# Attention mixing in four array quarters and two PSUM banks, with new order tables, in a fused recurrence and feed-forward kernel

## Chip, cores and metric

One core of a Trainium2 chip. The metric is the device time of one execution in microseconds, the median of three runs. Beside it there is one profiled execution, from which every row below comes. The engines are TensorE (PE; its weight loads are shown apart, PEld), VectorE (DVE), ScalarE (ACT), GpSimd (POOL) and SyncE (SP), which issues most DMAs.

## What is computed

A linear recurrence for each batch and head, then a feed-forward layer with a squared relu. All inputs are float32.

```python
# r, k, v, w: (B, H, S, D) = (4, 8, 768, 48); u: (8, 48)
for t in range(S):
    cur = einsum('bhd,bhe->bhde', u[None] * k[:, :, t], v[:, :, t])
    y[:, :, t] = einsum('bhd,bhde->bhe', r[:, :, t], state + cur)
    state = w[:, :, t, :, None] * state + einsum('bhd,bhe->bhde', k[:, :, t], v[:, :, t])
x = y.transpose(0, 2, 1, 3).reshape(B * S, H * D)          # (3072, 384)
h = maximum(x @ w_in, 0.0)                                 # w_in: (384, 2048)
out = h * h @ w_out                                        # w_out: (2048, 384)
```

## The kernel before

The time axis is cut into six chunks (c) of 128 steps. A chunk of one batch (b) is a unit; there are 24. The eight heads of a unit are four pairs (p): head j=0 of a pair lies in partitions 0 to 47, head j=1 in 64 to 111 (J = 64, HP = 112).

**Attention of a unit** (`attention`). The inputs w, k, r arrive in "st", v in "v". In chunk 0 TensorE transposes them (L466); later VectorE transposes 32x32 blocks and SyncE spreads them by DMA into "pt". VectorE takes the running product of w (L478), ScalarE its inverse (L485, L486), VectorE scales r and k by them. GpSimd and VectorE make beta, the diagonal term from u, and ScalarE writes it as diagonals into two "m" tiles (L515). TensorE makes the scores of each head into the two banks "a" (`scores`, L526), and VectorE copies them under a causal mask into the "m" tiles (L530). Then comes the mix: `inter` multiplies r by the state S (L552, from chunk 1 on) and `part` the masked scores by v (L560), both added up in one "a" bank. ScalarE and VectorE take the result out of the bank, negated and split into a rounded high part and a low rest (L591, L592), into x, the input of the feed-forward products. The 96 rows of pair 1 (`SPLIT`) don't fit beside the other three pairs in 128 partitions: they go to "x3", and six DMAs for each two units (`send`, L599) put them into the 16-row gaps of x. The transposed k (L538) times v gives the state's update (`outer`, L611, "dS"), added by VectorE and scaled by GpSimd (L617 to L620).

An L552 product has 48 rows of contraction and 48 or 64 output columns, so it uses a quarter of the 128x128 array: rows by the side of its head, columns by where its output lies. Before, head j=0 has the first row half and the first column half, j=1 the second of both: two of four quarters. L560 has all 128 rows and one column half. L526 has one row half and all columns.

**Feed-forward** (`ffn`). For each chunk and each of 16 slices (f) of 128 hidden values: nine products L640 (three blocks of 128 inputs, three pairings of high and low parts) into an "hp" bank, over 512 columns or, in chunk 0 and part of chunk 1, twice 256; relu on ScalarE, square on VectorE, high part on ScalarE, rest on VectorE (L645 to L649) into one of three "g" buffers; three products L655 for each batch, added up over all f in one of four "ob" banks. After the last f, ScalarE copies each "ob" to one of two "q" buffers (L660), and a DMA stores it (L662). The eight PSUM banks are thus four "ob", two "hp", two "a".

**Weights.** For each of eight groups, five DMAs bring the rows of w_in in the order that x needs (`load_w`), one brings w_out, and ScalarE, VectorE and GpSimd split them into high and low parts (`split_w`), through the same "q" buffers.

**Order.** Each piece is added to a `Plan` with an engine, a cost, a rank, and what it reads and writes. `Plan.order` is a list scheduler: of the steps that can start first, it takes the one of lowest rank, gives it buffers from named pools, and changes of the array's division cost `SWITCH`. The ranks come from the number tables in `Ranks`. In the first 110 us of the plan it fills TensorE's planned idle time with transposes of an identity (L681). The instructions are then emitted in that order, engine by engine.

**Flag.** Values of w far below the usual would make the fast path inexact; ScalarE adds up such cases in "far" (L518). After the plan, VectorE reduces it, a product with a 128x128 matrix of ones spreads it (L694), and every engine loads the result and branches over a slow path (L698) that does not run here.

## Time and profile before

| | |
|---|---|
| median of three runs | 550.34 us (550.27 to 550.54) |
| the profiled execution | 549.26 us, of which the span from first to last instruction is 547.3 |
| granted TensorE clock | 0.996 of full speed, mean over the span |
| DMA | 50.88 MB in 206456 packets, mean 93 GB/s |
| L640 products | 222.7 us busy |
| L655 products | 226.9 us busy |
| L526, L552, L560, L611 products | 28.3, 38.8 (21.5 + 17.3 by shape), 27.2 and 22.9 (12.4 + 10.5) us busy; these overlap each other in part |

A row of the profile's groups has the line, the engine, the operation, what it writes and reads, the shapes, the count, then the busy time in us and the mean of one in ns, then the idle time of the engine just before it and what ended that. In the timeline, a row has the start and the length in us of a run of like instructions, and in brackets the idle time before it. A matmul's end is modelled and lies after the start of the next one, so costs are best read from start to start. Weight loads overlap the products.

### The profile page before, as it was taken

To read this page: it belongs to the slowest core of one execution; us is meant where nothing else is said; L and a number is where in the kernel's file an instruction comes from. 1 tells how busy PE (TensorE), PEld (TensorE's weight loads), DVE (VectorE), ACT (ScalarE), POOL (GpSimd) and SP (SyncE) were. 2 spreads that over 40 slices of the span, in tenths; PEclk is the share of its full clock that TensorE was granted. 3 is DMA by queue.
4 is the path that set the end of the run, shared out by engine and by line. 5 is a ranking of instruction groups with operands and counts; after the bars stand their busy time and mean duration, and the time that the engine had idled before them with its cause. 6 is when DMAs were issued, how large, how long until landed. Compare 5 with 4: busy or idle time off the path is not lost. (4 is left out here: it accounts for less than half of the span.)

```text
span 547.3 us, 10350 instructions
## 1 busy us (share of the span) xinstructions
PE 532.6 (97%) x3930; PEld 474.5 (87%) x3930; DVE 357.1 (65%) x650; ACT 287.3 (52%) x677; POOL 102.3 (19%) x119
## 2 busy tenths in 40 slices
PE   7899999999999999999999999999999999999995
PEld 6778988889998989888888888888888889899994
DVE  5889989999587775958667747656855332333331
ACT  2886885566855845655643654545553332332322
POOL 5335653540212020210302002003000000000000
PEclk9999999999999999999999999999999999999998
DMA  9999699156563825455553723703411000000001
GB/s 164 216 244 272 128 245 206 24 90 136 115 132 64 169 47 105 97 104 99 101 107 62 138 73 60 142 3 73 74 57 30 1 0 16 29 31 1 0 1 62
DMA packets 206456, 50.88 MB, mean 93 GB/s; under 512 B 196161, under 2 KB 201281, under 8 KB 206401
## 3 DMA queue, kind: packets, MB, share of 16 engines
q1 hardware_dynamic: 205680, 49.17, 44.0%
q10 hardware_dynamic: 720, 0.98, 0.6%
q8 instruction: 33, 0.54, 0.4%
q14 instruction: 23, 0.18, 0.1%
HBM read 31.65 MB, written 4.72 MB: 66 GB/s over the span
## 5 line engine op out<-in xcount | busy, mean ns | idle before, releaser
L655 PE MATMUL ob<-wo,g 128*128 128x384 f32 x1152 | 226.9, 341 | 0.5 <-ACT g L648 0.5
L640 PE MATMUL hp<-x,wi 128*128 128x512 f32 (+1 forms) x1062 | 222.7, 355 | 1.4 <-DVE g L649 0.9
L655 PEld LDWEIGHTS ob<-wo,g 128*128 128x128 f32 x1152 | 199.3, 188 | 9.2 <-ACT g L648 0.7
L640 PEld LDWEIGHTS hp<-x,wi 128*128 128x128 f32 x1062 | 174.5, 188 | 27.5 <-DVE g L649 2.3
L645 ACT ACTIVATE t<-hp 128x512 f32<-128x512 f32 (+1 forms) x118 | 61.1, 518 | 154.2 <-PE hp L640 132.5
L646 DVE SCALAR_TENSOR_TENSOR hp<-hp,t 128x512 f32<-128x512 f32 (+1 forms) x118 | 70.3, 596 | 102.0 <-ACT t L645 101.5
L649 DVE TENSOR_TENSOR g<-hp,g 128x512 fp32r<-128x512 f32 (+1 forms) x118 | 68.9, 585 | 38.1 <-ACT g L648 37.3
L648 ACT CAST g<-hp 128x512 fp32r<-128x512 f32 (+1 forms) x118 | 59.5, 505 | 55.7 <-DVE hp L646 55.6
L515 ACT ACTIVATE m<-ident,beta 128x128 f32<-128x128 f32 x192 | 60.4, 395 | 1.2 <-DVE beta L508 1.2
L505 POOL TENSOR_TENSOR st<-st 128x384 f32<-128x384 f32 x24 | 26.6, 1108 | 61.7 <-DVE st L432 54.5
L620 POOL TENSOR_TENSOR S<-S,Ec 112x192 f32<-112x192 f32 x16 | 8.3, 523 | 142.2 <-DVE S L619 142.2
L530 DVE COPY_PREDICATED m<-caus,a 128x512 f32<-128x512 uint8 x48 | 33.3, 730 | 0.7 <-PE a L526 0.6
L478 DVE TENSOR_TENSOR_SCAN pt<-pt,zero 112x128 f32<-112x128 f32 x80 | 30.3, 426 | 3.0 <-DMA v<-in_v_dram 1.3
L526 PEld LDWEIGHTS a<-pt 48*128 48x128 f32 x384 | 23.6, 187 | 7.3 <-issue 5.1
L526 PE MATMUL a<-pt 48*128 48x128 f32 x384 | 28.3, 285 | 1.1 <-DVE pt L498 1.1
L560 PE MATMUL a<-m,v 128*48 128x128 f32 (+1 forms) x384 | 27.2, 279 | 1.0 <-DVE m L530 1.0
L432 DVE STREAM_TRANSPOSE st<-st 128x1152 f32<-128x1152 f32 x20 | 27.2, 1366 | 0.0
L560 PEld LDWEIGHTS a<-m,v 128*48 128x48 f32 (+1 forms) x384 | 20.0, 128 | 6.4 <-issue 4.6
L592 DVE SCALAR_TENSOR_TENSOR x<-a,x 112x128 fp32r<-112x128 f32 (+2 forms) x44 | 17.5, 431 | 12.3 <-ACT x L591 11.7
L507 POOL TENSOR_TENSOR st<-st,un 128x384 f32<-128x384 f32 x24 | 25.1, 1047 | 1.6
L404 POOL TENSOR_TENSOR wi<-q,wi 128x768 fp32r<-128x768 f32 x8 | 17.6, 2204 | 38.0 <-ACT wi L403 31.5
L495 DVE TENSOR_TENSOR pt<-pt,m 112x512 f32<-112x512 f32 x24 | 17.4, 728 | 8.9 <-ACT m L486 8.3
(78 smaller groups left out, 417.1 us busy)
## 6 DMA issues: line engine op xcount, KB each, us to landing
pt<-st SPq DMA_DIRECT2D x80, 96.0 KB, 2.3
ro<-in_moe_w_out_dram SPq DMA_DIRECT2D x8, 768.0 KB, 7.5
v<-in_v_dram SPq DMA_DIRECT2D x24, 192.0 KB, 3.4
st<-in_w_dram SPq DMA_DIRECT2D x11, 384.0 KB, 4.2
st<-in_k_dram SPq DMA_DIRECT2D x11, 384.0 KB, 5.4
st<-in_r_dram SPq DMA_DIRECT2D x11, 384.0 KB, 5.6
pt<-st SPq DMA_DIRECT2D x80, 48.0 KB, 2.5
out_dram<-q SPq DMA_DIRECT2D x20, 192.0 KB, 1.9
```

What stands on the lines that cost most here:

```text
L432: V.transpose(out=zt[:, i].rearrange("a t p q i -> a t (p q) i"), in_=sv[:, :, i].rearrange("s t p q x -> s t (p q) x"))
L478: lambda p=p: V.tensor_tensor_scan(out=pt[:, 0, p], data0=src(0)[:, p], data1=zero.broadcast_to([HP, C]), initial=1.0, op0=ALU.mult, op1=A ...
L515: A.activation(mv(j)[:, p], ident, AF.Copy, scale=beta.tile[:, 2 * p + j:2 * p + j + 1])
L526: T.matmul(mts[j].tile.rearrange("s (p t) -> s p t", p=NP)[:, p], pt[js, 2, p], pt[js, 1, p], start=True, stop=True)
L530: lambda j=j: V.copy_predicated(out=mv(j), mask=caus.unsqueeze(1).broadcast_to([128, NP, C]), data=mts[j].tile.rearrange("s (p t) -> s p t ...
L560: T.matmul(ybv()[to:to + n + D, spot(p)], vt.tile[:, o - n:o + D], mv(j)[:, p], start=(c == 0 and p == SPLIT), stop=True, skip_group_check ...
L640: T.matmul(hp.tile[:, 0:n], wi[f][:, wl, kt], xT[:, kt, xl, xs], start=(m == 0), stop=(m == 3 * KT - 1))
L645: P.add("act", 0.5 if full else 0.28, rank("g"), lambda: A.activation(t(), h(), AF.Relu), r=[hp], w=[(g, 1)])
L646: P.add("dve", 0.61 if full else 0.33, rank("g"), lambda: V.scalar_tensor_tensor(out=h(), in0=h(), scalar=0.0, in1=t(), op0=ALU.max, op1=A ...
L648: P.add("act", 0.53 if full else 0.31, rank("g"), lambda: A.copy(out=hi(), in_=h()), r=[hp], w=[(g, 0)])
L649: P.add("dve", 0.61 if full else 0.33, rank("g"), lambda: V.tensor_tensor(out=lo(), in0=h(), in1=hi().bitcast(F32), op=ALU.subtract), r=[h ...
L655: T.matmul(obs[b][:, 0:DM], g.tile[0][:, gl, o:o + C], wo[f][:, wl], start=(f == 0 and m == 0), stop=(f == NF - 1 and m == 2))
```

## The change

- The mix has two "a" banks (`yb`, `far_yb`) from chunk 1 on. Pairs 3 and 1 (`ACROSS`) put their heads' outputs in the other column half and into the second bank, so the eight L552 products of a unit go through all four quarters in turn. The outputs are taken out by three copies on each of ScalarE and VectorE in place of two and two, and `send` takes its rows from the other sides.
- The rows of w_in follow: the 96-row piece of each group is loaded as two of 48, so six DMAs in place of five, eight more in all. The slow path is adapted in the same way.
- The state update may only come after the mix (`after=[mixed]`).
- The planner lets a step ask ahead for slots that a later step will need (`claim`), and when a pool runs short it keeps the free place for the waiting step of lowest rank that lacks only that pool. The planned cost of the mix is 1.45 in place of 1.94.
- In the last chunk, the four results go to four "m" buffers; ScalarE copies batches 0 and 2, VectorE batch 1, and each half of batch 3; batches 0 and 2 are stored from ScalarE's queue, 1 and 3 from SyncE's.
- The flag is made by planned steps, with a product of one column, in place of steps after the plan.
- All tables in `Ranks` have new numbers.

```diff
-    AT = {'load': -105.75, 'z': 279.5, ...
-    LAG = 2
+    AT = {'load': -139.75, 'z': 137.75, ...
+    LAG = 74.5
...
+    ACROSS = (3, 1)
...
-        pieces = (..., (raw[PC:128 - PC, 2], rows[KT * R:KT * R + R]),
+        pieces = (...,
+                  (raw[PC:J, 2], rows[KT * R + D:KT * R + R]), (raw[J:HP, 2], rows[KT * R:KT * R + D]),
...
-        P.add("pe", 1.0, rank("mt"), scores, r=RK + KK, w=mts, mode=1)
+        P.add("pe", 1.0, rank("mt"), scores, r=RK + KK, w=mts, mode=1, claim=Ms)
...
         yb = Slot("a")
+        far_yb = Slot("a") if c else yb
+        side = lambda p, j: 1 - j if p in ACROSS else j
+        ahead = lambda p, j: PC if p in TILES and side(p, j) == 0 else 0
+        def spot(p):
+            if c == 0:
+                return ybv()[:, TILES.index(p) if p in TILES else KT]
+            return ybv(far_yb)[:, ACROSS.index(p)] if p in ACROSS else ybv()[:, TILES.index(p)]
         def inter():
-            for p in (*TILES, SPLIT):
+            for p in (0, 3, 2, 1):
                 for j in range(2):
-                    js, n = slice(j * J, j * J + D), ahead(p, j)
-                    T.matmul(ybv()[j * J:j * J + n + D, spot(p)], Ss[b][js, PC + p * D - n:PC + p * D + D], pt[js, 1, p],
-                             start=(spot(p) == 0), stop=False, skip_group_check=True)
+                    js, n, to = slice(j * J, j * J + D), ahead(p, j), side(p, j) * J
+                    T.matmul(spot(p)[to:to + n + D], Ss[b][js, PC + p * D - n:PC + p * D + D], pt[js, 1, p],
+                             start=(p in (0, 3)), stop=False, skip_group_check=True)
...
-            P.add("pe", 1.94, rank("mix"), mix, r=[vt, *Ms, ("S", b), *RK], w=[yb], mode=3)
-            outs = [("x", lambda: ybv()[0:HP, 0:KT], ..., xk, 0.4, 0.47),
-                    ("x3", lambda: ybv()[0:HP, KT], ..., (x3, ui), 0.18, 0.21)]
+            mixed = P.add("pe", 1.45, rank("mix"), mix, r=[vt, *Ms, ("S", b), *RK], w=[yb, far_yb], mode=3, claim=[x3])
+            outs = [("x", yb, lambda: ybv()[0:HP, 0:2], ..., xk + (0,), 0.3, 0.34),
+                    ("x", far_yb, lambda: ybv(far_yb)[0:HP, 0], ..., xk + (1,), 0.18, 0.21),
+                    ("x3", far_yb, lambda: ybv(far_yb)[0:HP, 1], ..., (x3, ui), 0.18, 0.21)]
...
-            P.add("pe", 0.5, rank("dS"), outer, r=[vt, Kt], w=[dS], mode=3)
+            P.add("pe", 0.5, rank("dS"), outer, r=[vt, Kt], w=[dS], mode=3, after=[mixed] if c else [])
...
-                os_ = Slot("q")
-                P.add("act", 0.4, rank("os"), ... A.copy(out=os_.tile[:, 0:DM], in_=obs[b][:, 0:DM]), r=[("ob", b)], w=[os_])
-                q_, e = ("actq", nc.scalar) if c == NC - 1 else ("sp", nc.sync)
+                end = c == NC - 1
+                os_ = Slot("m" if end else "q")
+                cut = DM // 2 if end and b == B - 1 else DM
+                if end and b % 2:
+                    P.add("dve", 0.45, rank("os"), ... V.tensor_copy(out=os_.tile[:, 0:cut], in_=obs[b][:, 0:cut]), ...)
+                else:
+                    P.add("act", 0.4, rank("os"), ... A.copy(out=os_.tile[:, 0:DM], in_=obs[b][:, 0:DM]), ...)
+                if cut < DM:
+                    P.add("act", 0.25, rank("os"), ... A.copy(out=os_.tile[:, cut:DM], in_=obs[b][:, cut:DM]), ...)
+                q_, e = ("actq", nc.scalar) if end and not b % 2 else ("sp", nc.sync)
...
+    P.add("dve", 0.2, rank, bad, r=[("far", c, b) for c in range(NC) for b in range(B)], w=["flag"])
+    P.add("pe", 0.2, rank, lambda: T.matmul(fps.tile[0:1, 0:1], flag, one, start=True, stop=True), r=["flag"], w=[fps])
...
-    fps = pas[0][:, 0:1]
-    T.matmul(fps, ones, flag, start=True, stop=True)
```

Three places in the order show what moves. The first is on TensorE, the L552 products of batch 1 in chunk 3 before (a_145 and a_146 are the two "a" banks, pt_127 holds the transposed r, S_130 the state of batch 1; the size is output rows by columns):

```order
L552 MATMUL a_146<-pt_127,S_130 64x128
L552 MATMUL a_146<-pt_127,S_130 48x128
L552 MATMUL a_146<-pt_127,S_130 64x128
L552 MATMUL a_146<-pt_127,S_130 48x128
L552 MATMUL a_146<-pt_127,S_130 64x128
L552 MATMUL a_146<-pt_127,S_130 48x128 x3
```

and the same eight products now, at line 564 of the changed kernel:

```order
L564 MATMUL a_145<-pt_127,S_130 64x128
L564 MATMUL a_145<-pt_127,S_130 48x128
L564 MATMUL a_146<-pt_127,S_130 48x128
L564 MATMUL a_146<-pt_127,S_130 64x128
L564 MATMUL a_145<-pt_127,S_130 64x128
L564 MATMUL a_145<-pt_127,S_130 48x128
L564 MATMUL a_146<-pt_127,S_130 48x128 x2
```

All eight went to one bank; now two go to one and two to the other in turn.

The second place is on TensorE too, behind the mix of the same unit: before, its last four L560 products (m are the masked scores, v_151 its v) and the first of a state update, that of batch 3 of chunk 2, whose v is v_152:

```order
L560 MATMUL a_146<-m_156,v_151 64x128
L560 MATMUL a_146<-m_158,v_151 48x128
L560 MATMUL a_146<-m_156,v_151 48x128
L560 MATMUL a_146<-m_158,v_151 48x128
L611 MATMUL a_145<-v_152,m_154 64x48
L611 MATMUL a_145<-v_152,m_154 48x48
L611 MATMUL a_145<-v_152,m_154 64x48
```

and now, the last of the mix of batch 1 (v_152) and the first of the state update of batch 0 (v_153); L668 is the former L655, L624 the former L611:

```order
L572 MATMUL a_146<-m_156,v_152 48x128
L572 MATMUL a_146<-m_155,v_152 48x128
L668 MATMUL ob_139<-wo_59,g_99 128x384 x3
L668 MATMUL ob_140<-wo_59,g_99 128x384 x3
L668 MATMUL ob_141<-wo_59,g_99 128x384 x3
L624 MATMUL a_145<-v_153,m_159 64x48
L624 MATMUL a_145<-v_153,m_159 48x48
```

A state update stood right behind the mix, in the bank that the mix left free; now nine feed-forward products on the undivided array stand between them. Through the whole order, TensorE goes from the undivided array to a divided form 60 times in place of 51, and between divided forms 25 times in place of 29. The identity transposes that fill idle time are 120 in place of 130, with 103 in place of 99 ahead of the first feed-forward product.

The third place is the end of ScalarE's work, before:

```order
L660 COPY q_147<-ob_139 128x384
L662 DMA out_dram<-q_147 128x384
L660 COPY q_148<-ob_140 128x384
L662 DMA out_dram<-q_148 128x384
L660 COPY q_147<-ob_141 128x384
L662 DMA out_dram<-q_147 128x384
L660 COPY q_148<-ob_142 128x384
L662 DMA out_dram<-q_148 128x384
```

and now (ob_139 to ob_142 are batches 0 to 3):

```order
L678 COPY m_155<-ob_139 128x384
L682 DMA out_dram<-m_155 128x384
L678 COPY m_157<-ob_141 128x384
L682 DMA out_dram<-m_157 128x384
L680 COPY m_156<-ob_142 128x192
```

Batch 1 and one half of batch 3 have gone to VectorE, and their two stores to SyncE's queue, where they are the last of the main program.

102 lines of the change are left out of this document (55 added, 47 removed).

## Prediction

> **What bounds the kernel now.** I read the page's busy times first, then the stretches of the span, then the waits of TensorE. On the page:
>
> ```profile
> span 547.3 us, 10350 instructions
> PE 532.6 (97%) x3930; PEld 474.5 (87%) x3930; DVE 357.1 (65%) x650; ACT 287.3 (52%) x677; POOL 102.3 (19%) x119
> ```
>
> TensorE is busy for 97% of the span, and no other engine for more than 65%. An average can hide stages, so the span is cut at 35, 100 and 541 us (columns: stretch, then busy time and count of TensorE, its weight loads, VectorE, ScalarE, GpSimd, then the granted clock, DMA share and GB/s):
>
> ```profile
> 0.00:35.00 35.00, 29.65 (x272) 24.89 (x272) 26.99 (x61) 21.43 (x54) 17.22 (x33) 1.00 1.05 207
> 35.00:100.00 65.00, 62.86 (x479) 55.94 (x480) 58.76 (x101) 49.10 (x105) 30.14 (x16) 1.00 0.88 199
> 100.00:541.00 441.00, 440.05 (x3182) 393.63 (x3182) 271.35 (x491) 215.79 (x517) 54.91 (x70) 1.00 0.34 68
> 541.00:547.30 6.30, 0.00 (x0) 0.00 (x0) 0.00 (x0) 0.96 (x2) 0.00 (x0) 0.62 0.31 104
> ```
>
> From 100 to 541 us TensorE is idle for 0.95 us in 441, at full clock: there, a microsecond of TensorE removed is a microsecond of span, as long as nothing new starves it. Before 35 us it idles for 5.35 us and also runs transposes that only fill idle time. After 541 us it has nothing left to do. So there are three stages with three limits: start, body, tail.
>
> ```profile
> L681 PE MATMUL a<-ident 128*128 128x128 f32 x97 | 15.0, 303 | 1.6 <-POOL ident masks.py:199 1.6
> L681 PE MATMUL hp<-ident 128*128 128x128 f32 x33 | 4.5, 276 | 0.0
> 12.21 4.31 PE L681 MATMUL a<-ident 128*128 128x128 f32 x38
> ```
>
> The fillers are 97 + 33 = 130; 38 in a row take 4.31 us, 0.113 us each, so 14.7 us of TensorE's "work" is idle time in disguise, all of it before 100 us.
>
> **The products with the state (body).** One unit in the middle of the body, in order of time (start, length, engine, line, operation, count; each float32 product shows as two records):
>
> ```profile
> 281.26 1.08 PE L552 MATMUL a<-pt,S 48*64 48x128 f32 x16
> 282.28 1.09 PE L560 MATMUL a<-m,v 128*64 128x128 f32 x16
> 283.19 0.62 PE L611 MATMUL a<-v,m 128*48 128x48 f32 x16
> 283.74 2.35 PE L655 MATMUL ob<-wo,g 128*128 128x384 f32 x12
> 285.94 2.26 PE L640 MATMUL hp<-x,wi 128*128 128x512 f32 x9
> ```
>
> From start to start, the 16 records of L552 take 1.02 us and those of L560, after which the array keeps its division, 0.91 us: 8 steps of 0.11 us, with two records in each. A record alone, the filler of the same 128 columns, also takes 0.113 us. So two quarters of the array already work side by side, and the other two are empty in L552 (48 rows by at most 64 columns each). How the pairs run:
>
> ```profile
> L552 PE MATMUL a<-pt,S 48*64 48x128 f32 x1 | 0.3, 320 | 0.0
> L552 PE MATMUL a<-pt,S 48*48 48x128 f32 x1 | 0.3, 307 | 0.0
> L611 PE MATMUL a<-v,m 128*64 128x48 f32 x8 | 0.6, 220 | 0.0
> L611 PE MATMUL a<-v,m 128*48 128x48 f32 x8 | 0.5, 208 | 0.0
> L611 PE MATMUL a<-v,m 128*64 128x48 f32 x2 | 0.3, 222 | 0.0
> ```
>
> The first two rows are the stretch 173.70 to 173.80 by shape: two products in different quarters have started there, although the first product's second record stands between them in the program. The next two are 177.68 to 178.30, eight records of each shape; the last is 178.20 to 178.22, where only the 64-column shape still runs. In the program the 48-column product comes last. So each division of the array takes its own products as fast as it can, past records that wait for another division. With four divisions I expect four records in a step: 4 steps in place of 8, 1.02 - 4 x 0.11 = 0.58 us, a gain of 0.44 us. Twenty units (chunks 1 to 5, four batches) have it: **20 x 0.44 = 8.8 us off**. Bounds: nothing if only two records ever run together; 10.2 us if the whole 1.02 us halves.
>
> Here two rules of the Trainium skill speak against the change. "TensorE: Matmul & The Clock Gate", section "The mechanism" under "Part 3: Packing small matmuls", says that matmuls start and end strictly in program order; by that, a third product would queue behind the second record of the first, and the gain would be 0. The trace does not agree: the 48-column shape of L611 was done while the 64-column one still ran. "TensorEngine Tiling (Array Packing)", "Gotcha 1: PSUM Pressure", says that row tiles cannot access one PSUM bank at the same time; by that, the two quarters that still share a bank would take turns, four records would need two steps, and again the gain would be 0. The trace does not agree here either: the two L552 records that started in one tenth of a microsecond are of the two row halves and write one bank.
>
> **More changes of the array's division (body).** The changed order takes the state update (L611) out of the mix's back and puts feed-forward products between them, as the rows on the change show. Counted through the whole order, TensorE leaves the undivided array 60 times in place of 51, and changes between divided forms 25 times in place of 29. The price, from these rows:
>
> ```profile
> 119.16 0.67 PE L611 MATMUL a<-v,m 128*64 128x48 f32 x16
> 119.76 2.36 PE L640 MATMUL hp<-x,wi 128*128 128x512 f32 x9
> 121.95 2.25 PE L655 MATMUL ob<-wo,g 128*128 128x384 f32 x12
> ...
> 441.87 2.26 PE L640 MATMUL hp<-x,wi 128*128 128x512 f32 x9
> 443.97 2.24 PE L655 MATMUL ob<-wo,g 128*128 128x384 f32 x12
> 446.06 2.26 PE L640 MATMUL hp<-x,wi 128*128 128x512 f32 x9
> 448.25 1.08 PE L552 MATMUL a<-pt,S 48*64 48x128 f32 x16
> 449.26 1.09 PE L560 MATMUL a<-m,v 128*64 128x128 f32 x16
> 450.28 2.03 PE L655 MATMUL ob<-wo,g 128*128 128x384 f32 x10
> ```
>
> Nine L640 take 2.10 us (441.87 to 443.97), but 2.19 before a divided group (446.06 to 448.25) and 2.19 after one (119.76 to 121.95): 0.09 each. L560 takes 0.91 before L611 and 1.02 before L655 (449.26 to 450.28): 0.11. L611 alone takes 0.60, not 0.55: 0.05. Together 0.34 per extra excursion, 9 x 0.34 = 3.0, less 4 x 0.09 for the inner changes: **2.6 us on**. If a third of the extra excursions lie in the start, where TensorE idles anyway, it is 1.7; 3.0 is the upper end.
>
> **Both banks for the mix (body).** The mix now needs both "a" banks, and three copies on ScalarE and three on VectorE empty them in place of two and two:
>
> ```profile
> L591 ACT ACTIVATE x<-a 112x384 fp32r<-112x384 f32 x20 | 9.7, 487 | 8.7 <-PE a L560 7.8
> L591 ACT ACTIVATE x<-a 112x128 fp32r<-112x128 f32 x20 | 5.4, 269 | 1.1 <-PE a L560 1.1
> L592 DVE SCALAR_TENSOR_TENSOR x<-a,x 112x384 fp32r<-112x384 f32 x20 | 11.1, 556 | 7.2 <-ACT x L591 6.7
> L592 DVE SCALAR_TENSOR_TENSOR x<-a,x 112x128 fp32r<-112x128 f32 x20 | 5.6, 282 | 3.5 <-ACT x L591 3.5
> ```
>
> Two of three blocks lie between the rows: about 0.38 us on ScalarE and 0.42 on VectorE. The first bank is free about 0.9 us after the mix, the second after about 0.38 + 0.42 + 2 x 0.28 = 1.4, with hand-overs 1.5. The extra 20 x 0.27 on each engine hides in their idle third and more of the body. What is queued on TensorE behind the mix is mostly feed-forward work that needs no such bank: in the changed order 2 to 5 us of it, 1.57 us (nine L655 of 0.174) in three or four units, 0.52 us in the first unit of chunk 1. I take one wait of 0.4 us and crumbs: **0.5 us on**. Ends: 0, and 3 us if every thin cover is missed by half a microsecond.
>
> **The start.** The order holds 120 fillers in place of 130, so the plan sees less idle time, though 103 in place of 99 ahead of the first feed-forward product. Ten fillers are **1.1 us off**. The splitting of one w_in piece adds eight DMA issues on SyncE's queue; the weights they bring are wanted tens of microseconds later, except the first. VectorE (26.99 of 35 us, then 58.76 of 65) is nearly as full as TensorE here, so the real order of waits decides: from 3 us off to 2 us on.
>
> **The tail.** ScalarE alone empties the last results, through two buffers:
>
> ```profile
> 534.12 6.43 PE L655 MATMUL ob<-wo,g 128*128 128x384 f32 x36
> 539.99 0.48 ACT L660 COPY q<-ob 128x384 f32<-128x384 f32 x1 [0.48 <-PE ob L655]
> 541.47 0.48 ACT L660 COPY q<-ob 128x384 f32<-128x384 f32 x1 [1.00 <-DMA out_dram<-q]
> 542.41 0.48 ACT L660 COPY q<-ob 128x384 f32<-128x384 f32 x1 [0.47 <-SPq L698]
> 542.92 1.02 ACTq L662 DMA_DIRECT2D out_dram<-q  x1
> out_dram<-q ACTq DMA_DIRECT2D x4, 192.0 KB, 2.3
> out_dram<-q SPq DMA_DIRECT2D x20, 192.0 KB, 1.9
> ```
>
> The last products end at 540.55. The third copy waits for the first buffer's DMA; the last issue starts at 542.92, lands by the median 2.3 us later (545.2), and 2.1 us of closing follow. With four buffers and two engines nothing waits for a landing: ScalarE copies batch 2 from about 540.05 to 540.53, issues its DMA until 540.9 (0.36 us, as at 539.53), copies its half of batch 3 until about 541.25 (VectorE's half is done before), and SyncE issues at 541.3, to land 1.9 to 2.3 later and end 2.1 after that: 545.3 to 545.7, so **1.7 us off**. If ScalarE's issue takes 1.02 us as the last one did, 1.0; if landing and closing shrink, 2.4. The flag's product and comparisons, planned into the body, leave a stretch in which they delayed nothing that ended last; I count them at nothing, and at 0.2 us on TensorE if uncovered.
>
> **Sum.** The profiled execution took 549.26 us: its span of 547.3 and 2.0 around it. -8.8 + 2.6 + 0.5 - 1.1 - 1.7 = -8.5, so 540.8. The median of the runs is 1.1 above the profiled one (550.34), which gives **541.8 us** in the median. A tie for a measurement of this kernel is what lies within 0.2%, 549.2 to 551.4.
>
> **Rivals.**
> - **Partial overlap.** Four quarters share one stream of instructions, and a step would have to take four weight loads. L611 issued its 16 records in 0.55 us, 0.034 each, which leaves four in 0.14 us, longer than a step of 0.11; against it, its 64-column shape set that pace. Half of the gain lost: 541.8 + 4.4 = 546.2.
> - **No overlap.** Only two records ever run together; the rows of before show no third. Then 541.8 + 8.8 = 550.6, a tie. (The two rules of the Trainium skill named above would give this.)
> - **Slower: the mix starves on its banks.** Scores before it and transposes behind it need the same two banks. If ScalarE's and VectorE's queues hold the six copies behind feed-forward work, TensorE waits at each mix. It is slower than before by 0.2% from (551.4 - 541.8) / 20 = 0.48 us per mix on; at the whole 1.5 us, it is 541.8 + 30 = 571.8. Against it: the body idles 0.95 us in all, ScalarE and VectorE about half and two fifths of it, and most mixes have 2 us of cover.
>
> **How the numbers follow.** Four quarters at once: 0.68, at 541.8; with the ends of the other terms taken together as roots of squares it reaches from 538.5 to 546. Partial: 0.14, at 546.2. None: 0.12, at 550.6. Starving: 0.06, above 551.4 in most of it. The range must hold 8 in 10: all of the first case but its lowest edge, and the partial one with its own spread, so 538 to 548. Faster by over 0.2%: 0.68 + 0.14 + 0.02 (no overlap, but a good start and tail) = 0.84; same 0.10; slower 0.06.
>
> **What would show it.** Right: L552's successor shows 16 records in about 0.58 us from start to start, and some tenth of a microsecond in which four of them start; TensorE idles under 2 us between 100 us and its end; 2.1 us of closing follow a landing about 3 us after the last product. Wrong on the overlap: the 16 records still take 1.0 us. Wrong on the banks: TensorE's waits name the copies of the mix or the masks. Wrong on the start: the first L640 begins more than 2 us away from its time of before, or fillers and idle time before 100 us add up to more than now.

## The result and the profile after

| | before | after |
|---|---|---|
| median of the runs on this chip | 550.44 us (550.27 to 551.28) | 546.89 us (545.78 to 547.37) |
| ratio of the two, 95% interval | | 0.993 [0.9915, 0.9946] |
| the profiled execution | 549.26 us, span 547.3 | 546.83 us, span 545.1 |

Faster by 0.7%: 3.55 us, where 8.5 were forecast. The time lies inside the forecast range, and well short of the forecast. The page after:

```profile
span 545.1 us, 10409 instructions
PE 525.9 (96%) x3920; PEld 462.0 (85%) x3920; DVE 361.2 (66%) x672; ACT 289.9 (53%) x696; POOL 103.0 (19%) x119
```

TensorE's busy time fell by 6.7 us and the span by 2.2: most of what was taken out of the products has come back as idle time. The span cut into start, body and tail as before (stretch, then busy time and count of TensorE, its weight loads, VectorE, ScalarE, GpSimd, then clock, DMA share, GB/s):

```profile
0.00:35.00 35.00, 28.73 (x271) 23.89 (x271) 28.07 (x59) 20.44 (x46) 18.27 (x33) 1.00 1.06 200
35.00:100.00 65.00, 61.29 (x467) 54.59 (x467) 60.41 (x102) 48.22 (x111) 26.45 (x16) 1.00 0.96 203
100.00:538.10 438.10, 435.89 (x3194) 383.48 (x3183) 272.42 (x512) 220.93 (x539) 58.30 (x70) 1.00 0.43 68
538.10:545.10 7.00, 0.01 (x1) 0.00 (x0) 0.36 (x1) 0.32 (x1) 0.00 (x0) 0.68 0.34 114
```

TensorE idles for 6.27 + 3.71 = 9.98 us before 100 us (7.49 before the change), for 2.21 in the body (0.95 before, of which 0.33 lie behind TensorE's last record, so 0.61 up to it) and for 7.0 in the tail (6.75, from the end of the last product at 540.55). The timeline of TensorE after, at the first mix with a state and at one in the middle (start, length, line, operation, count):

```profile
99.60 0.67 PE L564 MATMUL a<-pt,S 48*64 48x128 f32 x16
100.19 0.98 PE L572 MATMUL a<-m,v 128*64 128x128 f32 x14
...
300.80 2.25 PE L653 MATMUL hp<-x,wi 128*128 128x512 f32 x9
302.98 0.67 PE L564 MATMUL a<-pt,S 48*64 48x128 f32 x16
303.58 1.09 PE L572 MATMUL a<-m,v 128*64 128x128 f32 x16
304.60 0.72 PE L653 MATMUL hp<-x,wi 128*128 128x512 f32 x2
```

The 16 records of the products with the state (now L564) take 0.59 and 0.60 us from start to start, where they took 1.02; 0.58 was forecast. All four quarters run: the first four records start between 302.98 and 303.00. L572 takes 1.02 before an undivided product, as it did. TensorE's waits after (what waits, for whom, us in total, times, longest):

```profile
PE ob L472 <- DMA st<-in_w_dram: 2.2, 3, 1.3
PE a L572 <- DVE m L536: 1.9, 2, 1.1
PE hp L653 <- DVE g L662: 1.8, 4, 1.0
PE a L712 <- POOL ident masks.py:199: 1.6, 1, 1.6
PE a L472 <- DVE S L630: 1.3, 1, 1.3
```

All but the third are of the start: input transposes behind DMAs and behind the state in a bank they need, the mix of chunk 0 behind its mask, and the identity, which came as late before. The third is mostly of the body: feed-forward products behind g. Three of the same waits before:

```profile
PE ob L466 <- DMA st<-in_w_dram: 0.3, 1, 0.3
PE a L560 <- DVE m L530: 1.0, 2, 0.6
PE a L466 <- DVE S L617: 0.3, 1, 0.3
```

Where every microsecond of TensorE went, from the records of the two traces (from each product's start to the next one's, idle time taken out):

| TensorE, us | before | after | difference |
|---|---|---|---|
| r times state (L552, L564) | 20.28 | 12.37 | -7.9 |
| masked scores times v (L560, L572) | 23.87 | 25.26 | +1.4 |
| feed-forward products | 415.06 | 416.92 | +1.9 |
| state update and transposed k | 18.13 | 17.84 | -0.3 |
| fillers | 18.89 | 17.33 | -1.6 |
| idle, up to the last product | 6.49 | 10.59 | +4.1 |
| the flag's product | 0.28 | 0.12 | -0.2 |

The rest of TensorE's work differs by under 0.1. The sum is the 2.6 us by which TensorE's last record ends earlier (before, that is the flag's product).

### The profile page after: what moved, and what is told of

Same layout as the page of the kernel before. It is cut to its first block, busy times and chain, and to the rows that moved or that the text cites. A ratio compares the mean times of both kernels' runs of the same rounds, so it can differ in the third digit from the quotient of the medians.

```text
span 545.1 us, 10409 instructions
## 1 busy us (share of the span) xinstructions
PE 525.9 (96%) x3920; PEld 462.0 (85%) x3920; DVE 361.2 (66%) x672; ACT 289.9 (53%) x696; POOL 103.0 (19%) x119
## 4 chain that ended last, share of the span: by engine, by line
PE 75%; DVE 7%; DMA 6%; SPq 5%; ACT 4%; issue 1%; DVEq 0%
PE hp L653 32%; PE ob L668 31%; PE a L572 4%; PE a L532 3%; DMA ri<-in_moe_w_in_dram 2%; SPq L429 2%; SPq L448 2%; PE a L564 2%; DMA st<-in_w_dram 1%; PE a L624 1%; ACT m L521 1%; PE a L544 1%; DVE st L438 1%; DMA v<-in_v_dram 1%; DVE g L662 1%
## 5 line engine op out<-in xcount | busy, mean ns | idle before, releaser
L668 PE MATMUL ob<-wo,g 128*128 128x384 f32 x1152 | 221.4, 339 | 0.0
L668 PEld LDWEIGHTS ob<-wo,g 128*128 128x128 f32 x1152 | 198.5, 188 | 7.1 <-issue 2.0
L662 DVE TENSOR_TENSOR g<-hp,g 128x512 fp32r<-128x512 f32 (+1 forms) x118 | 68.8, 584 | 33.7 <-ACT g L661 31.7
L605 DVE SCALAR_TENSOR_TENSOR x<-a,x 112x128 fp32r<-112x128 f32 (+2 forms) x64 | 20.1, 344 | 31.4 <-ACT x L604 29.4
L511 POOL TENSOR_TENSOR st<-st 128x384 f32<-128x384 f32 x24 | 25.0, 1041 | 63.6 <-DVE st L438 62.5
L536 DVE COPY_PREDICATED m<-caus,a 128x512 f32<-128x512 uint8 x48 | 34.2, 731 | 4.1 <-PE a L532 4.1
L572 PE MATMUL a<-m,v 128*48 128x128 f32 (+1 forms) x384 | 27.5, 278 | 1.9 <-DVE m L536 1.9
L604 ACT ACTIVATE x<-a 112x128 fp32r<-112x128 f32 (+2 forms) x64 | 18.1, 322 | 19.6 <-PE a L572 18.1
L491 ACT ACTIVATE m<-pt 112x512 f32<-112x512 f32 x24 | 15.2, 633 | 24.6 <-DVE pt L484 20.5
L513 POOL TENSOR_TENSOR st<-st,un 128x384 f32<-128x384 f32 x24 | 26.6, 1112 | 1.8
L572 PEld LDWEIGHTS a<-m,v 128*48 128x48 f32 (+1 forms) x384 | 20.2, 128 | 6.9 <-issue 4.4
L410 POOL TENSOR_TENSOR wi<-q,wi 128x768 fp32r<-128x768 f32 x8 | 16.1, 2018 | 43.3 <-ACT wi L409 24.3
```

Of the source, the lines that this page charges most:

```text
L536: lambda j=j: V.copy_predicated(out=mv(j), mask=caus.unsqueeze(1).broadcast_to([128, NP, C]), data=mts[j].tile.rearrange("s (p t) -> s p t ...
L572: T.matmul(spot(p)[to:to + n + D], vt.tile[:, o - n:o + D], mv(j)[:, p], start=(c == 0 and p == SPLIT), stop=True, skip_group_check=True)
L662: P.add("dve", 0.61 if full else 0.33, rank("g"), lambda: V.tensor_tensor(out=lo(), in0=h(), in1=hi().bitcast(F32), op=ALU.subtract), r=[h ...
L668: T.matmul(obs[b][:, 0:DM], g.tile[0][:, gl, o:o + C], wo[f][:, wl], start=(f == 0 and m == 0), stop=(f == NF - 1 and m == 2))
```

## The experiments

Each kernel is the changed one with the edit that its diff shows, unless another is named. Each group of runs was taken on one chip, beside the kernel before; the chip differs between groups.

### First group: the same again, two quarters, the old tail, stores from ScalarE

**The changed kernel again**, without an edit.

> The changed kernel as it is, so that the others of this call have it on the same chip. Every theory: 546.9 within 0.5 us, 3.5 us under the kernel before.

Measured: 550.66 us median (548.8 to 553.82, 12 runs), before 550.57; ratio 0.9991 [0.9973, 1.0009]. Neither number was expected: on this chip the gain is gone, and the runs spread over 5 us. The mean granted clock of these runs goes from 0.982 to 0.992, that of the four first runs from 0.993 to 0.999, that of the kernel before from 0.993 up in nearly all of its runs. The windows of this run's start (the clock is the third number from the end):

```profile
20.00:25.00 5.00, 3.22 (x26) 2.14 (x24) 4.97 (x9) 2.59 (x6) 2.57 (x2) 0.85 1.18 164
25.00:30.00 5.00, 5.00 (x37) 4.28 (x35) 2.08 (x6) 2.89 (x7) 2.18 (x3) 0.50 1.04 248
...
45.00:50.00 5.00, 3.85 (x30) 2.80 (x30) 4.46 (x8) 4.34 (x10) 2.36 (x2) 0.74 1.00 265
50.00:55.00 5.00, 5.00 (x32) 4.56 (x30) 2.09 (x4) 2.38 (x8) 1.26 (x1) 0.58 1.06 257
```

and of the kernel before, whose start kept the full clock:

```profile
20.00:25.00 5.00, 4.28 (x56) 3.30 (x57) 4.62 (x7) 4.89 (x13) 1.55 (x1) 1.00 1.18 166
40.00:45.00 5.00, 4.41 (x59) 3.52 (x58) 4.62 (x9) 4.34 (x13) 2.52 (x1) 1.00 1.08 222
```

TensorE's clock is halved from 23.5 to 33.7 us and from 47.4 to 54.2, each time after idle time (20.5 to 22.0, and some 1.9 us in pieces between 44 and 46.5). A straight line through the 12 runs says 0.48 us more for each 0.001 of mean clock less (correlation -0.95), and 546.6 us at 0.997, beyond the highest clock among them. Lines through the runs of the kernel before in the first three groups say 550.4 to 550.9 there (one run at 0.947 left out). So with the clock held, the change gains about 4 us, and where it falls in most runs, as on this chip, nothing is left.

Why the same idle time halves the clock in one execution and not in another can be read from all 18 traces. Within a trace, all changes of the clock lie a whole number of 3.41 us apart, and this grid begins elsewhere in each execution (its first change is seen at 4.7 to 7.6 us). Cut at the grid, the 17 stretches in which TensorE idled for 1.73 us or more were all followed by half clock; none with up to 1.20 was; of the 25 between, seven were. Here the gap from 20.5 to 22.0 lies in one stretch, and 1.73 of its 3.41 us are idle:

```profile
20.08:23.49 3.41, 1.68 (x13) 0.89 (x11) 3.38 (x7) 2.51 (x6) 1.06 (x1) 1.00 1.07 165
23.49:26.90 3.41, 3.37 (x26) 2.74 (x27) 1.69 (x3) 0.31 (x1) 1.74 (x2) 0.50 1.26 206
```

In the first profile of the changed kernel a gap of nearly the same length (20.71 to 21.99) is cut in two by its grid at 21.84; 1.13 us fall into the first stretch, and the clock holds:

```profile
18.43:21.84 3.41, 2.28 (x21) 2.04 (x19) 3.41 (x6) 3.38 (x10) 0.00 (x0) 1.00 0.95 147
```

**Two quarters again:** the products keep their order and their two banks, the outputs go back to the own column half (all but pair 1 in chunk 0, where no product with the state is).

```diff
-        side = lambda p, j: 1 - j if p in ACROSS else j
+        side = lambda p, j: 1 - j if c == 0 and p == SPLIT else j
```

with the rows of w_in and of `send` to match.

> The changed kernel with its order, both banks and three copies, but with the state products back in two quarters (head j=0 always in the first column half, w_in rows and sends to match). Theory A, the four quarters give all that their rows show (0.43 us in each of 20 units) and the rest was lost elsewhere: 8.6 us above the changed kernel, about 555.5, with 1.0 us for 16 records. Theory B, the gain is given back because TensorE then waits for something else: 4 us or less above, about 551, with less idle time of TensorE than the changed kernel has between 100 us and its end.

Measured: 555.65 us (552.49 to 556.52), ratio to before 1.0075 [1.0049, 1.0101]. Its timeline:

```profile
279.52 1.08 PE L564 MATMUL a<-pt,S 48*64 48x128 f32 x16
280.53 1.09 PE L572 MATMUL a<-m,v 128*64 128x128 f32 x16
```

The 16 records take 1.01 us again, so the four quarters alone do it, not the second bank or the order. All of them take 20.49 us against 12.37. At a clock of 0.997 the lines through the runs give 552.8 against 546.6: of the 8.1 us that the rows show, 6.2 arrive in the time (5.0 by the medians). That lies between the two theories; 555.65 is theory A's figure only because the changed kernel itself took 3.8 us more here than the 546.9 that it starts from. TensorE idles 1.5 us less in the slower kernel (9.09 to 10.59): this fits theory B's reason, that where products get shorter, waits for others grow.

**The old tail:** the last results through two "q" buffers and ScalarE alone, as before.

> The changed kernel with the last results as before: two buffers, all four copies and stores on ScalarE. Theory A, the new tail is worth nothing, since it ends 7.0 us after the last product where the old one took 6.75: within 0.5 us of the changed kernel. Theory B, the forecast's 1.7 us are in it and the loss lies before: 1.7 us above the changed kernel, 548.6.

**Stores from ScalarE:** all four last stores from ScalarE's queue.

```diff
-                q_, e = ("actq", nc.scalar) if end and not b % 2 else ("sp", nc.sync)
+                q_, e = ("actq", nc.scalar) if end else ("sp", nc.sync)
```

> The changed kernel with all four last stores issued from ScalarE's queue, copies and buffers as changed. Theory A, SyncE's late stores hold up its jump over the slow path, which took 4 us on SyncE and VectorE after the last branch: the closing shrinks and the time is 1 to 3 us under the changed kernel. Theory B, the jump is slow for another reason: within 0.5 us of the changed kernel, SyncE again silent for about 4 us after its branch.

Measured: 550.56 us (546.82 to 553.3) and 549.19 (546.18 to 551.35); at 0.997, 546.1 and 546.4. Neither differs from the changed kernel by more than the lines can tell. From the last product's end to the span's end it is 6.7 and 6.3 us, against 6.8 in the changed kernel's profile of this group and 7.0 in its first: undoing the tail change changes nothing, although its last issue comes 3.05 us after the last product and not 0.77. With all stores from ScalarE, SyncE is past its branch at 481.8 us and nothing of it holds SyncE at the end: it goes on 0.02 us after each of the last two stores has landed. But these land 3.66 and 3.69 us after their issue, so the time is theory B's, and not for theory B's reason.

### Second group: the start

**Fillers where TensorE idled:** 37 more identity transposes, 10 and 11 ahead of two input transposes and 16 ahead of one mix of chunk 0.

```diff
+            if s.engine == "pe" and self.filler:
+                for _ in range({7: 10, 20: 11, 25: 16}.get(k, 0)):
+                    self.filler(s.fill[1] if k < 25 else self.spare)
+                k += 1
```

> The changed kernel once more, as the base for the three others of this call on the same chip. Theory A (the spread of its times comes from TensorE's granted clock in the start): times again from about 546 to 554, and the profile's mean clock and its time lie on one line with the earlier ones, 546.6 at 0.997 and 0.5 us more for each 0.001 less. Rival B (the spread is something of the chip, not of the kernel): spread under 1.5 us here, or a time off that line by over 1.5 us.

> The changed kernel with 37 more identity products (0.11 us each, 4.2 us in all) in the waits at 20 to 23 us and 37 to 43 us of the start, where TensorE idled in short pieces before its clock was halved. Theory A (the broken-up idle time lets the clock fall): the clock is 1.00 in every slice of 5 us before 100 us, the times lie within 1.5 us of each other at 546 to 547, about 3.5 us under the kernel before. Rival B (the fall has another cause): spread and median as in the changed kernel without them (550 with 546 to 554), and half clock is seen again. Rival C (the fillers stand in the way): clock held, but up to 4 us more in every run, 549 to 551.

Measured: the changed kernel again 549.2 us (545.9 to 552.06, 12 runs; ratio 0.9953 [0.9933, 0.9972]; 546.9 at 0.997, 0.44 us for each 0.001), with the fillers 548.6 (547.26 to 549.15, 7 runs; 0.9948 [0.9929, 0.9967]). The start of the run with fillers:

```profile
20.00:25.00 5.00, 4.36 (x47) 3.44 (x47) 4.83 (x9) 2.51 (x6) 2.64 (x2) 1.00 1.21 174
...
40.00:45.00 5.00, 4.78 (x52) 3.64 (x50) 5.00 (x9) 4.97 (x14) 1.81 (x1) 1.00 1.10 175
```

Without fillers, theory A: the same spread, and the profile (552.06 at 0.987) within 0.7 us of the line. With them, full clock up to 100 us in this profile, and a spread of 1.9 us in place of 6.2: fillers in the idle pieces hold the clock, though not always (of three profiles with them, one has half clock from 30.8 to 34.2). But the median is about 2 us over theory A's. Part of it are the fillers themselves (547.7 us at 0.997, 0.8 more than without), and half clock shows up in another place, in the body. TensorE and, below it, VectorE of the same run:

```profile
154.49 1.21 PE L673 MATMUL ob<-wo,g 128*128 128x384 f32 x6
157.97 2.29 PE L658 MATMUL hp<-x,wi 128*128 128x256 f32 x9 [2.27 <-DVE g L667]
160.06 1.16 PE L673 MATMUL ob<-wo,g 128*128 128x384 f32 x3
```

```profile
156.86 0.74 DVE L489 TENSOR_TENSOR_SCAN pt<-pt,zero 112x128 f32<-112x128 f32 x2 [2.51 <-DMA pt<-st]
157.52 0.40 DVE L667 TENSOR_TENSOR g<-hp,g 128x256 fp32r<-128x256 f32 x1
```

VectorE's scans of the next unit wait 2.51 us for the DMA of the transposed w; g, ready long before, is queued behind them; TensorE waits 2.27 us for g, and its next nine products take 2.09 us from start to start, at half clock, in place of 1.06.

**Fillers and stores from ScalarE.**

> As the one with 37 more identity products, and all four last stores issued from ScalarE's queue, so that SyncE has nothing to do after the last product. Theory A (the tail's 7 us are closing work that no copy or issue sets): within 0.5 us of the kernel with the same fillers. Rival B: 1 us or more under it, since the last issue follows the last copy on the same engine.

Measured: 548.1 us (545.52 to 549.14, 6 runs), ratio 0.9932 [0.9909, 0.9956]: as with the fillers alone, within what can be told. It is the lowest median of that group; its interval overlaps that of the changed kernel.

**The old start order:** the tables `U0`, `AT0`, `W0`, `WL` of before, all else new.

> The changed kernel with the four order tables that set the start (U0, AT0, W0, WL) as they were before; it holds 181 fillers and 64 excursions to a divided array. Theory A (the new start order costs the held clock and some 1.3 us more): clock 1.00 before 100 us, times within 1.5 us of each other; in the body the gain of the four quarters stays (20 x 0.42 = 8.4 us less on TensorE), and the time lies between 544 and 549, by how much the 61 more fillers (6.9 us at most) stand for idle time that was there before. Rival B (the start order is not what lowers the clock): half clock is seen in it too, and the times spread over 4 us or more.

Measured: 564.58 us, 1.0254 [1.023, 1.0279]: a miss for both theories. TensorE is busy for only 91.15 us of the 100 from 100 to 200 us, and at 100 to 105 us the clock falls to 0.72. The tables only fit together; half of each set is worse than either, and says nothing on the start alone.

### Third group: VectorE's queue, and the price of a division

**g ahead of the scans** at the two places in chunk 2 where TensorE waits for it (155 and 187 us), on VectorE alone but for one cast and one activation on ScalarE that change places. Rows of VectorE's order at the first place, t, hp and g being the feed-forward's, pt and m the next unit's:

```diff
-pt_127<-pt_127,zero 112x128 x2
 g_97<-hp_144,g_97 128x256
-pt_127<-pt_127,zero 112x128 x3
-pt_127<-pt_127 112x4x127
 hp_143<-hp_143,t_100 128x256
+g_99<-hp_143,g_99 128x256
+pt_127<-pt_127,zero 112x128 x5
+pt_127<-pt_127 112x4x127
```

> The changed kernel; at two places alone (units of batch 0 and 2 of chunk 2, about 155 and 187 us) VectorE does the square's rest g, the next square and the rest behind it ahead of the scans of the transposed w, which wait there for SyncE's DMAs. TensorE's, GpSimd's and SyncE's orders stay. Theory A (TensorE starves there because g is queued behind a scan that waits for a DMA): the waits of L653 for g, 1.4 us in the first profile of the changed kernel and 2.3 in the second chip's, fall under 0.4 us in all, no half clock is seen between 150 and 200 us, and the median falls by 1.5 to 2.5 us against the changed kernel (549.2 on the second chip), as far as the start's clock leaves it. Rival B (VectorE is late there anyhow, or the later scans make the scores late): as much waiting at other lines between 150 and 220 us, the time the same within 0.5 us.

Measured: 551.32 us (548.36 to 555.41), 1.002 [0.9993, 1.0047]; the runs at a clock of 0.997 and 0.998 took 548.4 to 548.9, some 2 us more than the changed kernel at that clock. TensorE's waits from 100 to 300 us:

```profile
PE hp L666 <- DVE g L675: 3.2, 3, 1.8
```

The rival holds in the waits; in time the swap is even some 2 us slower at the same clock. The wait at 155 us is gone, and 1.76 us stand at 162.8, 1.23 at 194.3: the scans and scalings, now later, stand ahead of the next g. Here no scan waits for a DMA: VectorE works without a break of over 0.2 us from 158.0 to 163.0, so the swap only moves the wait behind VectorE's own work. Whether an earlier landing of the transposed w would take it away was not tried.

**All of it together:** this swap, the fillers, and stores from ScalarE.

> The same two places of VectorE's order, the 37 more identity products of the start, and all four last stores from ScalarE's queue: what the runs so far call for, together. Theory A (half clock and starved products are the two sinks beside the sum): clock 0.996 or more in every run, median 545 to 546.2, spread under 1.5 us, 4.5 us or more under the kernel before. Rival B: they do not add up, 547 or more.

Measured: 548.26 us (547.82 to 550.54), 0.9951 [0.9936, 0.9966]. The rival again: no gain over the fillers and stores alone (548.1, on another chip), as the swap gives none. Five of six runs lie within 0.9 us.

**What a change of division costs:** 32 products of one column among chunk 5's feed-forward products, on 48x48 of the array or on all of it.

```diff
+                if c == NC - 1 and b % 2:
+                    T.matmul(pas[1][0:48, 0:1], ident[0:48, 0:48], ident[0:48, 0:1], start=True, stop=True)
```

> The changed kernel with 32 products of one column on 48x48 of the array, one in each half of the feed-forward steps of chunk 5 (between undivided products, into a bank nobody reads there): each is one more excursion to a divided array and back. Priced by the prediction (0.09 into, 0.11 out, and some 0.1 for what is not hidden of the weight load): 32 x 0.3 = 9.6 us between 430 us and the last product over the changed kernel's own. Rival (the price is that of a small product, not of the division): under 3 us, and the same as with 32 undivided products of one column.

> The changed kernel with 32 undivided products of one column (128x128) at the same 32 places: the small product alone, without a change of the division. By the prediction's pricing each costs a weight load that hides and a few columns: 0.02 to 0.11 each, 1 to 3.5 us in all, so 6 us or more under the divided ones. Rival: no difference between the two.

Measured: 563.47 and 557.27 us, both at a clock of 0.989, one run each, where the changed kernel takes 550.4 by its line from other chips: 13.1 and 6.9 more. The divided one, then the whole one:

```profile
538.41 0.25 PE L670 MATMUL a<-ident 48*48 48x1 f32 x2
538.59 1.33 PE L668 MATMUL ob<-wo,g 128*128 128x384 f32 x6
539.84 0.25 PE L670 MATMUL a<-ident 48*48 48x1 f32 x2
```

```profile
534.93 0.28 PE L670 MATMUL a<-ident 128*128 128x1 f32 x2
535.07 1.29 PE L668 MATMUL ob<-wo,g 128*128 128x384 f32 x6
536.20 0.28 PE L670 MATMUL a<-ident 128*128 128x1 f32 x2
```

From one small product to the next it is 1.43 us divided and 1.27 whole. So the excursion to the divided array and back costs 0.16 by these rows, 0.19 by the totals (6.2 / 32), provided that the two small products cost the same in themselves. Free of other chips and clocks is the stretch from chunk 5's first product with w_out to the end of its last: 60.5 us in the changed kernel, 72.6 divided, 67.3 whole. That is 12.1 more, where 9.6 were expected, and 6.8, where 1 to 3.5 were; 0.17 for the excursion and 0.21 for the small product, which the expectation put at 0.11 at most. Its "some 0.1" for a weight load that is not hidden is shown by no run alone. Neither rival holds.

### Fourth group: the branch at the end

One set of records was still unexplained. After the branch over the slow path, SyncE and VectorE of the changed kernel do nothing for 4 us; in the kernel before it was half a microsecond. From the records (start and end in us, engine, what it is; line 698 of before is 720 after):

```
before  541.765  541.810  SP   COMPARE_BRANCH
before  542.261  542.278  SP   EVENT_SEMAPHORE
after   539.047  539.119  DVE  COMPARE_BRANCH
after   539.263  539.308  SP   COMPARE_BRANCH
after   543.170  543.187  SP   EVENT_SEMAPHORE
after   543.304  543.325  DVE  EVENT_SEMAPHORE
```

**Without the slow path and its branch** (left out from `any_bad` on; the inputs here don't need it): the changed kernel, the changed kernel with the old tail, and the kernel before.

> The changed kernel without the slow path and the branch over it (the flag is still computed, but not loaded). Read is the tail: from the start of the last product to the end of the span, 7.0 to 7.35 us in four executions with the branch. Theory A (after the branch VectorE and SyncE stand still for 3.4 to 4.2 us, and that swallows what the four buffers gain): without it the last issue still comes 1.1 us after the last product, lands 2 to 2.8 later, and 1.9 of closing follow: a tail of 5.0 to 5.6 us. Rival B (landing and closing set the tail with or without it): 6.8 or more.

> The changed kernel with the last results through two buffers and ScalarE alone, as before, and without the slow path and its branch. Theory A (without the branch the two tails differ by what the prediction said, about 1.7 us): last issue 3.4 us after the last product, tail 6.6 to 7.2 us, 1.3 to 2 more than with four buffers. Rival B: the same tail as with four buffers within 0.4 us.

> The kernel before without the slow path and its branch. Theory A (before, the engines stood still for only 0.45 us after the branch, beside copies that ended later): tail 6.4 to 6.9 us against 6.9 with the branch. Rival B: a gain of 1 us or more, which would say that the branch already cost as much before.

Measured, in us: the tail from the last product's end to the span's end, and its three parts, from the last product's end to the last issue, from there to the landing of that store, and from the landing to the end. The last row is the kernel with all stores from ScalarE.

| | issue | landing | end | tail |
|---|---|---|---|---|
| four buffers, with the branch | 0.77 | 3.68 | 2.56 | 7.0 |
| without | 0.78 | 1.91 | 1.08 | 3.8 |
| two buffers, ScalarE alone, with the branch | 3.05 | 1.95 | 1.69 | 6.7 |
| without | 2.40 | 1.95 | 1.10 | 5.4 |
| before, with the branch | 2.37 | 2.64 | 1.73 | 6.75 |
| without | 2.37 | 1.88 | 1.10 | 5.35 |
| four buffers, all stores from ScalarE, with the branch | 0.92 | 3.69 | 1.70 | 6.3 |

From the start of the last product, as the expectations have it, each tail is 0.33 more. The kernels with the branch are those of the earlier profiles, on other chips; three profiles of the changed kernel have tails of 6.7 to 7.0.

The rows of TensorE and the spans for the four buffers without the branch:

```profile
core 0 of [0], span 546.2 us
534.97 7.47 PE L668 MATMUL ob<-wo,g 128*128 128x384 f32 x42
```

and for the two buffers without it, with ScalarE's last copy and issue:

```profile
core 0 of [0], span 547.3 us
534.71 7.12 PE L668 MATMUL ob<-wo,g 128*128 128x384 f32 x40
...
543.72 0.48 ACT L673 COPY q<-ob 128x384 f32<-128x384 f32 x1 [0.47 <-DMA out_dram<-q]
544.23 0.34 ACTq L675 DMA_DIRECT2D out_dram<-q  x1
```

The last products end at 542.44 and 541.83. Theory A holds in kind: without the branch the four buffers gain 1.67 us, the 1.7 of the forecast; with it they gain nothing, because the branch costs 3.2 us there and 1.25 with the old tail. The two tails themselves, 4.1 and 5.8 from the start of the last product, are shorter than theory A's 5.0 to 5.6 and 6.6 to 7.2. Before, the branch cost 1.4, which was the rival of the third of these runs.

The 3.2 us are of two kinds. The end comes 1.5 us sooner after the landing: SyncE does not stand still, and there is less to close (1.1 us against 1.7 where SyncE waits for the landing). And the last store lands 1.8 us sooner. While it is in flight with the branch (538.8 to 542.6 us), two queues fetch instructions (queue: packets, MB, share of the 16 engines' time); the last row is the store itself, with the time to its landing at the end. Then the same store without the branch:

```profile
q8 instruction: 1, 0.02, 2.3%
q14 instruction: 3, 0.02, 1.7%
out_dram<-m SPq DMA_DIRECT2D x1, 192.0 KB, 3.7
```

```profile
out_dram<-m SPq DMA_DIRECT2D x1, 192.0 KB, 1.9
```

In all traces, every one of the four last stores that took over 2.2 us to land (up to 4.0) was in flight during a fetch of 16 KB; without the branch there is none in the tail, and all twelve stores land after 1.8 to 2.0. That the fetch delays the stores is likely, but not shown apart from the branch.

The whole times of the three kernels without the branch are 547.94, 549.06 and 550.69 us, one run each, at clocks of 0.990, 0.989 and 0.994, beside 549.69 at 0.997 for the kernel before. The changed kernel was not run on this chip, so the gain is shown in the tail and not in the whole time.

**The flag computed after the plan, as before:**

```diff
-    P.add("pe", 0.2, rank, lambda: T.matmul(fps.tile[0:1, 0:1], flag, one, ...), r=["flag"], w=[fps])
+    T.matmul(fps, ones, flag, start=True, stop=True)
```

> The changed kernel with the flag computed after the plan, as before: the product with the 128x128 ones behind the last feed-forward product, and SyncE's and VectorE's loads of it behind that. Theory A (the planned flag is what turned 0.45 us of standing still after the branch into 4): under 1 us again after the branch on SyncE and VectorE, and a tail of 5.5 to 6.5 us. Rival B (it is the last copies and stores on VectorE and SyncE, or the branch's place in the code): 2.5 us or more again, and a tail of 7 us or more.

Measured: 3.0 us of silence on both engines, a tail of 7.0 (547.51 us, one run). The rival holds: it isn't the planned flag. Here the last store lands 1.91 us after its issue, at 541.46, and SyncE goes on only at 543.86: standing still behind the branch is enough by itself for a tail of 7.0, as late stores are by themselves for one of 6.3 in the kernel with all stores from ScalarE.

## Why the prediction was right and wrong, point by point

| term | forecast | measured on the profiled execution |
|---|---|---|
| four quarters | -8.8 | -7.9 |
| more changes of the division | +2.6 | +3.0 |
| waits in the body, both banks | +0.5 | +1.6 |
| start, idle time and fillers | -1.1 | +0.9 |
| tail | -1.7 | +0.25 |
| sum, on the profiled execution | -8.5 | -2.4 |
| from there to the median | +1.1 | +0.1 |

The measured terms come to -2.2 of span; 0.2 more lie around it. (The body's 1.6 is from 0.61 to 2.21 us of idle time, up to the last product.)

- **Four quarters: right, in mechanism and nearly in size.** Four records run in a step, 0.60 us a unit, and four start within 0.02 us; undoing it alone brings 1.01 back. By this case's records the products of different quarters neither go in strict program order nor take turns on a bank: the two rules of the Trainium skill that were weighed would have left 1.0 us.
- **Divisions: right in sum and near in its parts, but not in the price of one excursion.** The feed-forward products take 1.9 us more (9 x 0.18 = 1.6 in the prediction), the masked scores times v 1.4 (9 x 0.11 = 1.0): in 11 units a state update followed them, and they took 0.92 us, now 1.02 before an undivided product. The transposed k and the state update take 0.3 less (0.1 more). But an excursion put in on purpose costs 0.16 to 0.19 us where 0.34 were priced; it is of one small product and not of a whole mix, so the two don't exclude each other, and what makes up the rest stays open.
- **Banks: the fear was right in kind, the place wrong.** No wait names the copies of the mix; the masks are named, for 0.5 us at two products with the state in the body. What grew most is the wait for g behind VectorE's scans, which wait for a DMA of SyncE's queue; in this execution 1.4 us in two places, 0.44 at 156.1 and 0.97 at 187.3 us, 2.2 and 2.3 in the changed kernel's profiles of the next two groups. TensorE idles 2.21 us from 100 us to its end, where under 2 was the sign of being right.
- **The start: the step that failed first.** "Ten fillers are 1.1 us off" read the plan's fillers as the measure of idle time. The fillers fell as counted, and unplanned waits took their place: the fillers' time fell by 1.6 us, but TensorE's idle time before 100 us rose by 2.5, from 7.49 to 9.98 us, and the first feed-forward product moved from 34.71 to 37.14. Both signs that the prediction named for being wrong on the start came. The waits that grew are those for the input w (0.3 to 2.2 us), for the mask of chunk 0 (1.0 to 1.9) and for the state (0.3 to 1.3); which table causes them is not shown, as the only run on it fits no theory. The prediction's range "3 us off to 2 us on" held the 0.9. What it had no term for is the clock: those same waits halve it in most executions on the two other chips, by where the grid of 3.41 us falls, which costs another 2 to 4 us there.
- **The tail: the other step that failed, by as much.** "With four buffers and two engines nothing waits for a landing" is true: the last issue came at 538.88, 0.77 us after the last product, as laid out. What failed is "to land 1.9 to 2.3 later and end 2.1 after that": the store landed 3.68 us later, at 542.56, and the end came 2.56 after that, since SyncE, which does the closing, stood still behind the branch until 543.17. Without the branch it is 1.91 and 1.08, and the gain is there in full. The prediction took both as constants from one execution. Its 2.3 was the median of 1.9, 1.8, 3.1 and 2.6 us, and the last two of these, which set the end, were in flight during a fetch of instructions; its 2.1 follows from that median, and was really 1.7. It never asked what the branch asks of the other engines once ScalarE is not the last to finish.
- **The median:** the 1.1 us between the profiled execution and the median of before did not recur. By luck this made the miss smaller, 5.1 us in place of 6.0. That the range held the result is luck too: the case of four quarters was to reach 546 at most, and 546.89 lies in the part of the range that was there for a partial overlap, which did not occur.

What stays open: why the branch at the end is followed by about 0.5 us of silence on SyncE and VectorE before, and by 2.5 to 4.2 in the kernels with the new order. It isn't the planned flag; nor is it SyncE's last stores (with all from ScalarE, VectorE is still silent for 3.3 us); the length and place of the code were not tried. Open too is what decides on the clock between 1.2 and 1.7 us of idle time in a stretch of the grid.

## What to carry to other kernels

A term that moves the last work of a kernel must be followed to its very end on every engine: what ends last once this engine no longer does? Fillers planned into idle time measure the plan's idle time, not the chip's: count the real waits around them, and where they break TensorE's work for 1.2 us or more within 3.4, price the clock as well. And repeat the run on another chip before a gain under one per cent is believed: this one was 0.7%, 0.1% and 0.5% on three.

## What the runs showed of the hardware

- **Half clock after short waits.** In the traces the clock fell to 0.50 within 2 us after TensorE had idled 1.5 to 1.8 us at a stretch (20.5 to 22.0 us, full again at 33.7; 189.3 to 191.1, full again at 195.0), or some 2 us in pieces (42.1 to 44.5, half from 44.8 to 48.2), and stayed there for 3.4, 6.8 or 10.2 us. In these 18 traces it goes by the idle time within one stretch of a grid of 3.41 us that each execution begins elsewhere: from 1.73 us on always, up to 1.20 never. The Trainium skill ("TensorE: Matmul & The Clock Gate", section "Why this matters for your kernels") asks for no idle gaps over about 3 us between bursts; here gaps of half that length were enough.
- **A branch can cost 3 us at the end of a kernel**, though it is taken in 0.05 to 0.07: in the kernels with the new order VectorE, and SyncE where it branches in the tail, issued nothing for 2.5 to 4.2 us behind it, ScalarE resumed after 0.1 to 0.4. Instructions were fetched by DMA in that time (packets of up to 16 KB on the instruction queues), and the last stores landed up to 4.0 us after their issue, not 1.8 to 2.0. Leaving the branch and the code behind it out took 1.25 to 3.2 us off the tail.
- **A product of one column is not free**: 0.21 us among feed-forward products, for two records.
